# Talking-heads attention and two MLPs on one core: one shuffle transfer for each block of ten tokens, loads issued by GpSimd, deeper weight buffers

## The chip, the core and the metric

The kernel runs on one core of a Trainium2 chip. The metric is the device time of one execution, in microseconds. TensorE (PE) multiplies, VectorE (DVE), ScalarE (ACT) and GpSimd (POOL) work on tiles, and SyncE (SP) issues transfers. Each engine executes its own instructions in program order; transfers run on 16 DMA engines.

## The reference, cut to what matters

```python
def _attn_ref(q, k, v, w_pre, w_post):          # 4 batches, 12 heads, 448 tokens, 64 wide
    scores = scale * np.matmul(q, k.transpose(0, 1, 3, 2))
    scores = np.einsum('bhij,hg->bgij', scores, w_pre)     # mixes the heads
    scores = scores - np.max(scores, axis=-1, keepdims=True)
    attn = np.exp(scores)
    attn = attn / (np.sum(attn, axis=-1, keepdims=True) + 1e-09)
    attn = np.einsum('bhij,hg->bgij', attn, w_post)        # mixes the heads again
    return np.matmul(attn, v)
# x = attention output as (1792, 768); then
# _moe_ref:  h = x @ w_in (768x1024); h * softmax(h); layer norm; @ w_out
# _moe2_ref: relu(x @ w_in (768x2048))**2 @ w_out
```

## The kernel before, in words

The program has three parts: attention, the first MLP and the second MLP. The change touches attention, and the conversion of the first MLP's weights that is interleaved with it.

**Chunks and blocks.** The 448 tokens of a batch are cut into chunks of 120, 120, 120 and 88. A chunk's scores are computed for one pair of heads at a time (`qk`, six calls a chunk): tokens go to partitions 0 to 59 (first half of the chunk) and 64 to 123 (second half), and ACT copies the result to `ssrc`, whose row on a partition holds 12 heads by 448 keys. To mix the heads, partitions must become (token, head) pairs. So `shuffle` sends a block of ten tokens (`R = 10`) from `ssrc` to a tile `sdst`: five tokens of the first half by one transfer of 60 rows, five of the second half by another. Each row is 448 float32. A slot treats two blocks. There are 180 blocks and 90 slots.

**A slot s** issues, in this order: the loads whose turn it is (k, q, v, raw weights), the shuffles of slot s+5 (`DS = 5`), stores of converted weights, `pre(s+2)` on PE (the first head mix), `post_out(s-1)` on DVE (from PSUM to `at`), `qk` for a later chunk, `negmax` and `expo` of slot s+2, `av` (the product with v) where a chunk has just been completed, `weigh(s+1)` (the reciprocal of the sums on DVE, the scaled weights `w` on GpSimd), and `post(s)` on PE (the second head mix). `qk`, `av` and `post` share two PSUM buffers, `ring`.

**Weights.** `load_w1` fetches 48 pieces of 128 by 256 int64 words to `w1raw` (3 buffers). `narrow` turns a piece into float32 with one ACT instruction (L76) and four DVE instructions (L77, L81, L85, L89); they are placed singly between the other DVE instructions by `filler()`. The result is in `w1t` (3 buffers), from which `store_w1` sends it to DRAM. Every load, shuffle and store above is issued by SP. A piece i is loaded in slot (3i+7)//2, its conversion is queued in slot (3i+8)//2, and its store is issued in slot (3i+16)//2.

**Startup.** GpSimd clears small tiles, among them `wz`, which 16 warm-up matmuls read; then come the six `qk` of the first chunk.

Of the kernel before, what the change touches and what calls it, by code (L numbers as in the profile page):

```python
# [18 lines left out]
def kernel(  # L19
# [40 lines left out]
    w1iD = dram.tile([DM, F1], F32, name="w1iD")  # L60
    w1oD = dram.tile([F1, DM], F32, name="w1oD")

    mask_sb = const.tile([128, RH], F32, name="mask_sb")
    wp_raw = const.tile([128, H], F32, name="wp_raw")
    wq_raw = const.tile([128, H], F32, name="wq_raw")
    wpre_bd = const.tile([128, 64], F32, name="wpre_bd")
# [59 lines left out]
    blocks = []  # L126
    for b in range(B):
        for (i0, n) in CHUNKS:
            c, nb, oa = len(chunks), -(-n // R), 0
            chunks.append(dict(b=b, i0=i0, n=n, first=len(blocks), nb=nb))  # L130
            for k in range(nb):
                r = len(range(k, n, nb))
                blocks.append((c, k, r, oa))
                oa += r
# [13 lines left out]
    def load_k(b, g):  # L148

        t = early_p.tile([128, KG, S], F32, tag=f"k{g}", name="k", bufs=2)  # L150
        src = kT[b].rearrange("p (a d) s -> d (p a) s", a=2)
        for e in range(2):
            o = e * HP + KG * g
            nc.sync.dma_start(out=t[64 * e:64 * e + 64], in_=src[:, o:o + KG])
        kk[b, g] = t

    def load_q(c):
# [9 lines left out]
    def load_v(b, j):  # L167
        if j < NJ:
            t = late_p.tile([JW, H, D], F32, tag=f"v_{j}", name="v", bufs=2)
            nc.sync.dma_start(out=t, in_=v[b, j * JW:(j + 1) * JW].rearrange("j (g d) -> j g d", g=H))  # L170
        else:
            t = late_p.tile([128, 2, G2, D], F32, tag=f"v_{j}", name="v", bufs=2)
            src = v[b, j * JW:S].rearrange("j (e g d) -> e j g d", e=2, g=G2)
            for e in range(2):
                nc.gpsimd.memset(t[64 - 64 * e:128 - 64 * e, e], 0.0)
            for e in range(2):
                nc.sync.dma_start(out=t[64 * e:64 * e + 64, e], in_=src[e])
        vv[b, j] = t

    def qk(c, p, dve=0):  # L180


        ch = chunks[c]
        n, half = ch["n"], RH * ch["nb"]
        if c not in ssrc:
            ssrc[c] = ss_p[c % 2].tile([128, H, S], F32, tag="ssrc", name="ssrc")
        ps = ring()
        k = kk[ch["b"], p // KG]
        for x in range(2):
            for e in range(2):  # L190
                u = x ^ e
                nc.tensor.matmul(  # L192
                    out=ps[64 * u:64 * u + 64, e, 0:S],
                    lhsT=qq[c][64 * e:64 * e + 64, p * n + u * half:p * n + u * half + 64],
                    rhs=k[64 * e:64 * e + 64, p % KG],
                    start=True,
                    stop=True,
                )
        (nc.vector.tensor_copy if dve else nc.scalar.copy)(ssrc[c][:, p:H:HP, :], ps[:, :, 0:S])  # L199

    def rows(t, u):

        return H * (RH if u == 0 else blocks[t][2] - RH)

    def shuffle(t):
        c, k, r, oa = blocks[t]
        nb = chunks[c]["nb"]
        d = late_p.tile([128, S], F32, tag="sdst", name="sdst", bufs=10)
        for u in range(2):
            m = rows(t, u)  # L210
            o = 64 * (u ^ (t % 2))
            f = 64 * u + k
            nc.sync.dma_start(out=d[o:o + m], in_=ssrc[c][f:f + (m // H - 1) * nb + 1:nb])
        sdst[t] = d
# [7 lines left out]
    def pre(s):  # L222

        ps = [psb_p.tile([128, 512], F32, tag="pre", name="ps_pre", bufs=4) for b in range(2)]
        ds = [sdst.pop(2 * s + b) for b in range(2)]
        for b, r in ((0, 0), (0, 1), (1, 0), (1, 1)):
            u = r ^ b
            m = rows(2 * s + b, u)
            nc.tensor.matmul(  # L229
                out=ps[b][64 * u:64 * u + 64, 0:S],  # L230
                lhsT=wpre_bd[64 * r:64 * r + m],
                rhs=ds[b][64 * r:64 * r + m],
                start=True,
                stop=True,
            )
        pres[s] = ps
# [41 lines left out]
    def post(s):  # L278

        ps = ring()  # L280
        w = ws.pop(s)
        for b in range(2):
            e = es.pop((s, b))
            for j in range(NJ + 1):
                for x in range(2):
                    for u in range(2):
                        c = x ^ u
                        m = rows(2 * s + b, u)
                        o = j * JW + c * 64 if j < NJ else NJ * JW
# [11 lines left out]
    def post_out(s, b):
        c, k, r, oa = blocks[2 * s + b]
        ps = pps[s] if b == 0 else pps.pop(s)
        if c not in at:
            at[c] = late_p.tile([128, NU, 120], F32, tag="at", name="at", bufs=2)
        nc.vector.tensor_copy(  # L306
            at[c][:, :, oa:oa + R].rearrange("p n (u i) -> p u n i", u=2),
            ps[:, :, b * NU * RH:(b + 1) * NU * RH].rearrange("p u (n i) -> p u n i", i=RH),
        )

    def av(c, a):

        ch = chunks[c]
        n, nb = ch["n"], ch["nb"]
# [16 lines left out]

        kf = n - (R - 1) * nb
        pv = ps[:, 0, 0:360].rearrange("p (q t) -> p q t", q=3)
        for k0, k1, i1 in ((0, kf, R), (kf, nb, R - 1)):
            if k0 == k1:
                continue
            o = k0 * R
            nc.scalar.copy(
                xt[c][:, 3 * a:3 * a + 3, 0:i1 * nb].rearrange("p q (i k) -> p q k i", k=nb)[:, :, k0:k1],
                pv[:, :, o:o + (k1 - k0) * i1].rearrange("p q (k i) -> p q k i", i=i1),  # L340
            )
        if a == 1:
            at.pop(c)

# [15 lines left out]

    def load_w1(i):
        src, dst, k, o = w1pieces[i]
        t = raw_p.tile([128, WP], I64, tag="w1raw", name="w1raw", bufs=3)
        nc.sync.dma_start(out=t, in_=src[k * 128:(k + 1) * 128, o:o + WP])
        w1raw[i] = t

    def narrow_w1(i):
        src, dst, k, o = w1pieces[i]
        sq = raw_p.tile([128, WP], F32, tag="w1sq", name="w1sq", bufs=1)
        t = raw_p.tile([128, WP], F32, tag="w1t", name="w1t", bufs=3)  # L370
        yield from narrow(w1raw.pop(i), sq, t)
        if dst is w1oD:
            nc.scalar.activation(out=t, in_=t, func=AF.Copy, scale=g_sb[:, k:k + 1])
# [86 lines left out]
    nc.gpsimd.memset(mask_sb, 0.0)  # L460
    nc.gpsimd.memset(wp_raw, 0.0)
    nc.gpsimd.memset(wq_raw, 0.0)
    for u in range(2):
        nc.sync.dma_start(out=mask_sb[64 * u:64 * u + PR], in_=mask[0:PR, 0:RH])
        nc.sync.dma_start(out=wp_raw[64 * u:64 * u + PR], in_=w_pre.unsqueeze(0).to_broadcast([RH, H, H]))
    load_q(1)
    for u in range(2):
        nc.sync.dma_start(out=wq_raw[64 * u:64 * u + PR], in_=w_post.unsqueeze(0).to_broadcast([RH, H, H]))

    def consts():  # L470
# [3 lines left out]
        nc.vector.tensor_tensor(  # L474
            out=wpre_bd[:, 0:PR].rearrange("p (i g) -> p i g", g=H),
            in0=wp_raw.unsqueeze(1).to_broadcast([128, RH, H]),
            in1=mask_sb.unsqueeze(2).to_broadcast([128, RH, H]),
            op=ALU.mult,
        )
        nc.vector.tensor_tensor(  # L480
            out=wpost_bd,
            in0=wq_raw.unsqueeze(2).to_broadcast([128, H, RH]),
            in1=mask_sb.unsqueeze(1).to_broadcast([128, H, RH]),
            op=ALU.mult,
        )

# [502 lines left out]
```

## Time and profile before

| | |
|---|---|
| median of 3 runs | 1217.07 us (1215.13 to 1221.67) |
| the profiled execution: time, span | 1219.8 us, 1218.0 us |
| mean granted TensorE clock | 0.943 of full speed |
| PE, DVE, ACT, GpSimd busy, share of the span | 90%, 58%, 39%, 17% |
| attention | about the first 480 us |
| the two MLPs | the rest; PE is busy nearly all of it |

An engine's busy share is an average over the whole span, and the parts differ. What a change in attention is worth has to be read from that part alone, by the waits inside it.

### The profile page before, as it was taken

To read this page: it belongs to the slowest core of one execution; us is meant where nothing else is said; L and a number is where in the kernel's file an instruction comes from. 1 tells how busy PE (TensorE), PEld (TensorE's weight loads), DVE (VectorE), ACT (ScalarE), POOL (GpSimd) and SP (SyncE) were. 2 spreads that over 40 slices of the span, in tenths; PEclk is the share of its full clock that TensorE was granted. 3 is DMA by queue.
4 is the path that set the end of the run, shared out by engine and by line. 5 is a ranking of instruction groups with operands and counts; after the bars stand their busy time and mean duration, and the time that the engine had idled before them with its cause. 6 is when DMAs were issued, how large, how long until landed. Compare 5 with 4: busy or idle time off the path is not lost.

```text
span 1218.0 us, 31090 instructions
## 1 busy us (share of the span) xinstructions
PE 1099.0 (90%) x12920; PEld 937.2 (77%) x12920; DVE 710.8 (58%) x1419; ACT 473.8 (39%) x1033; POOL 211.3 (17%) x362
## 2 busy tenths in 40 slices
PE   8587877776786797999999999999999999999998
PEld 2354544454454475788899899999999999999998
DVE  2465755565566665483344268737676766666734
ACT  4354545455555555342122135633223232232211
POOL 0101111011111125260111035401111111111100
PEclk8878988888989896999999999999999999999999
DMA  4565556455655545231111046402111112111113
GB/s 138 166 187 175 171 185 190 161 170 187 195 168 190 175 148 186 71 98 46 52 48 38 20 150 193 125 27 66 53 52 53 53 52 60 54 57 52 40 66 117
DMA packets 103895, 135.01 MB, mean 111 GB/s; under 512 B 21835, under 2 KB 87243, under 8 KB 103755
## 3 DMA queue, kind: packets, MB, share of 16 engines
q1 hardware_dynamic: 102154, 132.38, 34.6%
q8 instruction: 102, 1.67, 0.6%
q10 hardware_dynamic: 1600, 0.64, 0.2%
q14 instruction: 39, 0.31, 0.1%
HBM read 71.65 MB, written 22.81 MB: 78 GB/s over the span
## 4 chain that ended last, share of the span: by engine, by line
PE 56%; DVE 1%; DMA 1%; ACT 0%; POOL 0%; issue 0%; SPq 0%; DVEq 0%; POOLq 0%
PE ps_h L853 19%; PE ps_y L892 19%; PE ps_o L699 10%; PE ps_h L429 8%; PE ps_tr L685 1%; DMA x2r<-x2D 1%; DMA xD<-xt 0%; DVE e L668 0%; PE ps_ye L892 0%; ACT x L762 0%; ACT y L901 0%; DVE x L764 0%; DVE st L661 0%; DVE e L658 0%; POOL x L764 0%
## 5 line engine op out<-in xcount | busy, mean ns | idle before, releaser
L853 PE MATMUL ps_h<-x,ti 128*128 128x384 f32 (+1 forms) x1440 | 241.9, 325 | 0.0
L892 PE MATMUL ps_y<-to,g 128*128 128x384 f32 x1332 | 240.7, 337 | 0.9 <-ACT y L901 0.9
L853 PEld LDWEIGHTS ps_h<-x,ti 128*128 128x128 f32 x1440 | 236.8, 188 | 0.0
L892 PEld LDWEIGHTS ps_y<-to,g 128*128 128x128 f32 x1332 | 232.5, 188 | 3.0 <-DVE y L903 1.7
L292 PEld LDWEIGHTS ps_ring<-w,e 60*64 60x64 f32 (+1 forms) x5760 | 104.4, 144 | 95.9 <-issue 65.5
L292 PE MATMUL ps_ring<-w,e 60*64 60x60 f32 (+2 forms) x5760 | 111.9, 228 | 49.7 <-DVE at L306 30.0
L306 DVE COPY at<-ps_ring 128x420 f32<-128x420 f32 x180 | 105.1, 605 | 87.4 <-PE ps_ring L292 86.7
L192 PE MATMUL ps_ring<-k,q 64*64 64x448 f32 x768 | 109.6, 602 | 50.2 <-DVE at L306 49.1
L199 ACT COPY ssrc<-ps_ring 128x896 f32<-128x896 f32 x93 | 84.2, 906 | 127.1 <-PE ps_ring L192 99.0
L247 ACT ACTIVATE e<-ps_pre,nm 128x448 f32<-128x448 f32 x180 | 113.4, 637 | 45.7 <-DVE nm L240 43.6
L861 ACT ACTIVATE r<-ps_h 128x384 f32<-128x384 f32 (+1 forms) x80 | 37.5, 469 | 214.1 <-PE ps_h L853 214.0
L699 PE MATMUL ps_o<-zt,w1o 128*128 128x384 f32 (+1 forms) x720 | 120.2, 326 | 0.0
L429 PE MATMUL ps_h<-w1i,xs 128*128 128x512 f32 x504 | 120.1, 395 | 0.0
L324 PEld LDWEIGHTS ps_ring<-at,v 128*64 128x64 f32 x1536 | 89.9, 158 | 35.6 <-issue 21.4
L699 PEld LDWEIGHTS ps_o<-zt,w1o 128*128 128x128 f32 x720 | 117.1, 189 | 0.0
L240 DVE TENSOR_REDUCE nm<-ps_pre 128x1 f32<-128x448 f32 x180 | 107.3, 613 | 12.9 <-PE ps_pre L229 12.9
L862 DVE SCALAR_TENSOR_TENSOR r<-ps_h,r 128x384 f32<-128x384 f32 (+1 forms) x80 | 42.4, 530 | 122.6 <-ACT r L861 122.6
L192 PEld LDWEIGHTS ps_ring<-k,q 64*64 64x64 f32 x768 | 35.0, 145 | 101.8 <-issue 77.5
L264 POOL TENSOR_TENSOR w<-wpost_bd,sm 128x60 f32<-128x60 f32 x166 | 44.3, 288 | 389.1 <-DVE sm L259 202.0
L903 DVE TENSOR_TENSOR y<-ps_y,y 128x768 f32<-128x768 f32 x97 | 92.4, 952 | 32.0 <-PE ps_y L892 32.0
L229 PE MATMUL ps_pre<-sdst,wpre_bd 60*64 60x448 f32 x720 | 106.2, 603 | 4.8 <-DMA sdst<-ssrc 4.0
L429 PEld LDWEIGHTS ps_h<-w1i,xs 128*128 128x128 f32 x504 | 94.1, 188 | 21.3
(77 smaller groups left out, 1064.8 us busy)
## 6 DMA issues: line engine op xcount, KB each, us to landing
sdst<-ssrc SPq DMA_DIRECT2D x352, 105.0 KB
wr<-in_moe_w_in_dram SPq DMA_DIRECT2D x32, 384.0 KB
wr<-in_moe_w_out_dram SPq DMA_DIRECT2D x32, 384.0 KB
w1raw<-in_moe_w_in_dram SPq DMA_DIRECT2D x24, 256.0 KB
w1raw<-in_moe_w_out_dram SPq DMA_DIRECT2D x24, 256.0 KB
k<-in_kT_dram SPq DMA_DIRECT2D x24, 224.0 KB
out_dram<-y SPq DMA_DIRECT2D x13, 384.0 KB
v<-in_v_dram SPq DMA_DIRECT2D x12, 384.0 KB
```

Of the source, the lines that this page charges most:

```text
L192: nc.tensor.matmul(out=ps[64 * u:64 * u + 64, e, 0:S], lhsT=qq[c][64 * e:64 * e + 64, p * n + u * half:p * n + u * half + 64], rhs=k[64 * ...
L229: nc.tensor.matmul(out=ps[b][64 * u:64 * u + 64, 0:S], lhsT=wpre_bd[64 * r:64 * r + m], rhs=ds[b][64 * r:64 * r + m], start=True, stop=True,)
L240: nc.vector.tensor_reduce(out=nm, in_=pres[s][b][:, 0:S], op=ALU.max, axis=AX.X, negate=True)
L247: nc.scalar.activation(out=e, in_=pres[s][b][:, 0:S], func=AF.Exp, bias=nms.pop((s, b)), scale=1.0, accum_out=sms[s][:, b:b + 1])
L292: nc.tensor.matmul(out=ps[64 * c:64 * c + 64, u, i0:i0 + ng * RH], lhsT=e[64 * u:64 * u + m, o:o + 64], rhs=w[64 * u:64 * u + m, b, g0:g0 ...
L306: nc.vector.tensor_copy(at[c][:, :, oa:oa + R].rearrange("p n (u i) -> p u n i", u=2), ps[:, :, b * NU * RH:(b + 1) * NU * RH].rearrange(" ...
L324: nc.tensor.matmul(out=ps[64 * e:64 * e + 64, 0, q * 120:q * 120 + n], lhsT=t[:, g] if j < NJ else t[:, e, p], rhs=at[c][:, j * H + (g if ...
L429: nc.tensor.matmul(out=ps[:, u], lhsT=t[:, a, cc], rhs=w1i[cc][:, w, u * 512:(u + 1) * 512], start=(cc == 0 and a == 0 and w == 0), stop=( ...
L699: nc.tensor.matmul(out=ps[:, 0:width], lhsT=w1o[k][:, w, cc * 128:(cc + 1) * 128], rhs=zT[:, a, k, 0:width], start=(k == 0 and i == 0), st ...
L853: nc.tensor.matmul(out=ps[:, 0:n], lhsT=ti[:, w, cc, f * 128:(f + 1) * 128], rhs=x2[q][:, a, cc], start=(cc == 0 and i == 0), stop=(cc == ...
L892: nc.tensor.matmul(out=ps[:, u - us[0], 0:DM // 2], lhsT=g[:, a, f, o:o + 128], rhs=to[:, w, f, u * (DM // 2):(u + 1) * (DM // 2)], start= ...
L903: nc.vector.tensor_tensor(out=yo, in0=po, in1=yo, op=ALU.add)
```

## The change

A block's ten tokens now come from one half of a chunk. A block therefore needs one transfer of 120 rows, from ten partitions of `ssrc` to partitions 4 to 123 of `sdst`. Rows 0 to 3 are cleared once for ten fixed tiles, and the first head mix reads 64 rows instead of 60 for one of its two products. Because the place of the tokens in PSUM after `post` is another, `post_out` copies one bank for both blocks of a slot instead of both banks for one block, and `av` orders its output accordingly; where two blocks differ in chunk or size, `post_out` makes two copies of half the size. The loads of v, of the raw weights, and of k from the second batch on are issued by GpSimd. `w1raw` has 5 buffers instead of 3, `w1t` 6 instead of 3, and a piece is loaded two or three slots earlier, in slot (3i+2)//2.

```diff
+            n0 = 60 if n == 120 else 50
+            for u, m in enumerate((n0, n - n0)):
+                nk = -(-m // R)
+                for k in range(nk):
+                    r = len(range(k, m, nk))
+                    blocks.append((c, 64 * u + k, nk, r, oa))
...
-            nc.sync.dma_start(out=t[64 * e:64 * e + 64], in_=src[:, o:o + KG])
+            (nc.gpsimd if b else nc.sync).dma_start(out=t[64 * e:64 * e + 64], in_=src[:, o:o + KG])
...
-            nc.sync.dma_start(out=t, in_=v[b, j * JW:(j + 1) * JW].rearrange("j (g d) -> j g d", g=H))
+            nc.gpsimd.dma_start(out=t, in_=v[b, j * JW:(j + 1) * JW].rearrange("j (g d) -> j g d", g=H))
...
+    gaps = []
+    for i in range(10):
+        d = late_p.tile([128, S], F32, name=f"sdst{i}")
+        nc.gpsimd.memset(d[0:4], 0.0)
+        gaps.append(d)
...
     def shuffle(t):
-        c, k, r, oa = blocks[t]
-        nb = chunks[c]["nb"]
-        d = late_p.tile([128, S], F32, tag="sdst", name="sdst", bufs=10)
-        for u in range(2):
-            m = rows(t, u)
-            o = 64 * (u ^ (t % 2))
-            f = 64 * u + k
-            nc.sync.dma_start(out=d[o:o + m], in_=ssrc[c][f:f + (m // H - 1) * nb + 1:nb])
+        c, f, nk, r, oa = blocks[t]
+        d = gaps[t % 10]
+        nc.sync.dma_start(out=d[4:4 + r * H], in_=ssrc[c][f:f + (r - 1) * nk + 1:nk])
         sdst[t] = d
...
-            m = rows(2 * s + b, u)
+            m = H * size(2 * s + b, 1) if r else 64
...
+    def post_out(s, u):
+        ps = pps[s] if u == 0 else pps.pop(s)
+        pv = ps[:, u, 0:2 * NU * RH].rearrange("p (b n i) -> p b n i", b=2, i=RH)
+        two = [blocks[2 * s + b] for b in range(2)]
...
+        if c0 == c1 and r0 == r1 == R:
+            dst = at[c0][:, :, oa:oa + 2 * R].rearrange("p n (x i) -> p x n i", i=RH)
+            nc.vector.tensor_copy(dst[:, 1:3] if u else dst[:, 0:4:3], pv)
+        else:
+            for b, (c, f, nk, r, oa) in enumerate(two):
+                g = u ^ b
+                m, o = size(2 * s + b, g), oa + RH * g
+                nc.vector.tensor_copy(at[c][:, :, o:o + m], pv[:, b, :, 0:m])
...
-        t = raw_p.tile([128, WP], I64, tag="w1raw", name="w1raw", bufs=3)
-        nc.sync.dma_start(out=t, in_=src[k * 128:(k + 1) * 128, o:o + WP])
+        t = raw_p.tile([128, WP], I64, tag="w1raw", name="w1raw", bufs=5)
+        nc.gpsimd.dma_start(out=t, in_=src[k * 128:(k + 1) * 128, o:o + WP])
...
-        t = raw_p.tile([128, WP], F32, tag="w1t", name="w1t", bufs=3)
+        t = raw_p.tile([128, WP], F32, tag="w1t", name="w1t", bufs=6)
...
-        at_slot((3 * i + 7) // 2, load_w1, i)
+        at_slot((3 * i + 2) // 2, load_w1, i)
```

Where the instructions stand now: on SP, in the first batch (`sdst` is a shuffle, `w1iD<-w1t` a store of converted weights, `xD<-xt` a store of the attention output). Before:

```order
L213 DMA sdst<-ssrc 60x1x448 x4
L350 DMA xD<-xt 64x6x120 x2
L164 DMA q<-in_qT_dram 64x720 x2
L364 DMA w1raw<-in_moe_w_in_dram 128x256
L213 DMA sdst<-ssrc 60x1x448 x4
L381 DMA w1iD<-w1t 128x256
```

The same place with the change:

```order
L401 DMA w1iD<-w1t 128x256
L214 DMA sdst_94<-ssrc 120x1x448
L214 DMA sdst_96<-ssrc 120x1x448
L370 DMA xD<-xt 64x6x120 x2
L168 DMA q<-in_qT_dram 64x720 x2
L214 DMA sdst_98<-ssrc 120x1x448
L214 DMA sdst_100<-ssrc 120x1x448
L401 DMA w1iD<-w1t 128x256
```

Four shuffles a slot have become two, and the loads of raw weights have left this queue.

On GpSimd, in the middle of the first batch (`w` are the scaled weights of the second head mix), before:

```order
L264 TENSOR_TENSOR w<-wpost_bd,sm 128x60 x2
L175 MEMSET v 64x384 x2
L264 TENSOR_TENSOR w<-wpost_bd,sm 128x60 x10
L161 MEMSET q 128x64
L264 TENSOR_TENSOR w<-wpost_bd,sm 128x60 x10
```

With the change:

```order
L179 MEMSET v 64x384 x2
L181 DMA v<-in_v_dram 64x384 x2
L269 TENSOR_TENSOR w<-wpost_bd,sm 128x60 x2
L384 DMA w1raw<-in_moe_w_in_dram 128x256
L269 TENSOR_TENSOR w<-wpost_bd,sm 128x60 x2
L158 DMA k<-in_kT_dram 64x2x448 x2
L384 DMA w1raw<-in_moe_w_in_dram 128x256
L269 TENSOR_TENSOR w<-wpost_bd,sm 128x60 x2
```

One to three transfers now stand ahead of a slot's two products `w`.

On GpSimd at the start of the program, with the change:

```order
L208 MEMSET sdst_110 4x448
L208 MEMSET sdst_112 4x448
L468 MEMSET wz 128x256
L165 MEMSET q 128x64
L479 MEMSET wpre_bd 128x64
```

Ten clears of 4 by 448 (the last two are shown) now stand ahead of `wz`, which was the first of them before.

## Rows read from the trace of the kernel before

**Rows 1.** Stretches of the span: busy time and instructions of each engine, clock, DMA share.

```profile
core 0: us, PE busy (x) PEld busy (x) DVE busy (x) ACT busy (x) POOL busy (x), PEclk, DMA share, GB/s
14.00:26.00 12.00, 9.82 (x52) 2.91 (x52) 3.06 (x8) 4.53 (x8) 0.00 (x0) 0.72 0.30 109
...
14.00:478.00 464.00, 352.36 (x8344) 225.84 (x8344) 270.05 (x727) 245.75 (x567) 62.93 (x207) 0.86 0.55 175
...
498.00:1218.00 720.00, 714.50 (x4112) 689.38 (x4106) 427.98 (x664) 216.49 (x440) 140.05 (x133) 1.00 0.22 69
```

**Rows 2.** Issues on SP by line: count, ns min/median/max, first and last start.

```profile
L213 SPq DMA_DIRECT2D sdst<-ssrc x360: 665/742/881, 13.9 to 470.8; - x180
L364 SPq DMA_DIRECT2D w1raw<-in_moe_w_in_dram x24: 362/522/1540, 42.0 to 227.3; - x24
L154 SPq DMA_DIRECT2D k<-in_kT_dram x24: 607/656/1467, 2.0 to 319.8; - x24
```

**Rows 3.** Timeline of SP's queue, 386 to 396 us: start, duration, what.

```profile
386.09 3.58 SPq L213 DMA_DIRECT2D sdst<-ssrc  x4
389.72 0.47 SPq L381 DMA_DIRECT2D w1oD<-w1t  x1
...
390.89 0.45 SPq L364 DMA_DIRECT2D w1raw<-in_moe_w_out_dram  x1
391.58 3.63 SPq L213 DMA_DIRECT2D sdst<-ssrc  x4
395.26 0.46 SPq L381 DMA_DIRECT2D w1oD<-w1t  x1
```

**Rows 4.** Timeline 395 to 398 us: start, duration, what, idle time before it.

```profile
395.57 0.29 DVE L77 TENSOR_SCALAR w1t<-w1raw 128x256 uint32<-128x256 uint32 x1 [7.26 <-DMA w1oD<-w1t]
...
397.36 1.77 PE L192 MATMUL ps_ring<-k,q 64*64 64x448 f32 x8 [9.35 <-DVE at L306]
```

**Rows 5.** Waits of DVE and ACT for transfers, first 480 us: total, times, longest.

```profile
DVE w1t L77 <- DMA w1oD<-w1t: 33.9, 10, 8.5
DVE w1t L77 <- DMA w1iD<-w1t: 30.2, 7, 6.7
DVE w1t L77 <- DMA w1raw<-in_moe_w_in_dram: 14.9, 3, 8.9
...
ACT ssrc L199 <- DMA sdst<-ssrc: 18.7, 6, 7.9
ACT w1sq L76 <- DMA w1raw<-in_moe_w_in_dram: 16.1, 5, 8.4
ACT w1sq L76 <- DMA w1raw<-in_moe_w_out_dram: 7.9, 4, 4.2
```

**Rows 6.** Timeline of PE, 233 to 243 us, between two stalls.

```profile
233.24 2.68 PE L324 MATMUL ps_ring<-at,v 128*64 128x120 f32 x48
235.85 1.13 PE L292 MATMUL ps_ring<-w,e 60*64 60x60 f32 x64
...
239.64 1.13 PE L292 MATMUL ps_ring<-w,e 60*64 60x60 f32 x64
240.56 0.99 PE L229 MATMUL ps_pre<-sdst,wpre_bd 60*64 60x448 f32 x8
241.34 0.96 PE L192 MATMUL ps_ring<-k,q 64*64 64x448 f32 x8
242.42 1.13 PE L292 MATMUL ps_ring<-w,e 60*64 60x60 f32 x64
```

**Rows 7.** Timeline of the start: GpSimd's first clears and PE's first `qk`.

```profile
0.73 0.31 POOL L448 MEMSET wz<- 128x256 f32 x1 [0.29 <-POOLq L975]
0.97 0.15 POOL L161 MEMSET q<- 128x64 f32 x1
...
6.13 2.17 PE L192 MATMUL ps_ring<-k,q 64*64 64x448 f32 x16
```

**Rows 8.** GpSimd's largest wait, first 480 us: total, times, longest.

```profile
POOL w L264 <- DVE sm L259: 202.0, 39, 13.1
```

More of the change, by code (lines that the diff above doesn't have):

```diff
@@ L61 @@
     w1oD = dram.tile([F1, DM], F32, name="w1oD")
-    mask_sb = const.tile([128, RH], F32, name="mask_sb")
+    mask_sb = const.tile([128, 2, RH], F32, name="mask_sb")
     wp_raw = const.tile([128, H], F32, name="wp_raw")
@@ L128 @@
         for (i0, n) in CHUNKS:
[L129 to L134, printed above, removed]
+            c, oa = len(chunks), 0
+            n0 = 60 if n == 120 else 50
+            chunks.append(dict(b=b, i0=i0, n=n, first=len(blocks), n0=n0))
+            for u, m in enumerate((n0, n - n0)):
[3 more added lines that the diff above has]
+                    blocks.append((c, 64 * u + k, nk, r, oa))
+                    oa += r
+            chunks[c]["nb"] = len(blocks) - chunks[c]["first"]
     NB = len(blocks)
@@ L176, in load_v @@
             for e in range(2):
-                nc.sync.dma_start(out=t[64 * e:64 * e + 64, e], in_=src[e])
+                nc.gpsimd.dma_start(out=t[64 * e:64 * e + 64, e], in_=src[e])
         vv[b, j] = t
@@ L183, in qk @@
         ch = chunks[c]
-        n, half = ch["n"], RH * ch["nb"]
+        n, half = ch["n"], ch["n0"]
         if c not in ssrc:
@@ L199, in qk, with size @@
         (nc.vector.tensor_copy if dve else nc.scalar.copy)(ssrc[c][:, p:H:HP, :], ps[:, :, 0:S])
-    def rows(t, u):
-        return H * (RH if u == 0 else blocks[t][2] - RH)
-    def shuffle(t):
-        c, k, r, oa = blocks[t]
-        nb = chunks[c]["nb"]
-        d = late_p.tile([128, S], F32, tag="sdst", name="sdst", bufs=10)
-        for u in range(2):
-            m = rows(t, u)
-            o = 64 * (u ^ (t % 2))
-            f = 64 * u + k
-            nc.sync.dma_start(out=d[o:o + m], in_=ssrc[c][f:f + (m // H - 1) * nb + 1:nb])
+    gaps = []
[3 more added lines that the diff above has]
+        gaps.append(d)
+    def shuffle(t):
+        c, f, nk, r, oa = blocks[t]
+        d = gaps[t % 10]
+        nc.sync.dma_start(out=d[4:4 + r * H], in_=ssrc[c][f:f + (r - 1) * nk + 1:nk])
         sdst[t] = d
+    def size(t, g):
+        return RH if g == 0 else blocks[t][3] - RH
     es = {}
@@ L287, in post @@
                         c = x ^ u
-                        m = rows(2 * s + b, u)
+                        m = H * size(2 * s + b, u ^ b)
                         o = j * JW + c * 64 if j < NJ else NJ * JW
@@ L299, in post @@
         pps[s] = ps
[L301 to L309, printed above, removed]
+    def post_out(s, u):
+        ps = pps[s] if u == 0 else pps.pop(s)
+        pv = ps[:, u, 0:2 * NU * RH].rearrange("p (b n i) -> p b n i", b=2, i=RH)
+        two = [blocks[2 * s + b] for b in range(2)]
+        for c, f, nk, r, oa in two:
+            if c not in at:
+                at[c] = late_p.tile([128, NU, 120], F32, tag="at", name="at", bufs=2)
+        (c0, _, _, r0, oa), (c1, _, _, r1, _) = two
+        if c0 == c1 and r0 == r1 == R:
[6 more added lines that the diff above has]
+                nc.vector.tensor_copy(at[c][:, :, o:o + m], pv[:, b, :, 0:m])
     def av(c, a):
         ch = chunks[c]
-        n, nb = ch["n"], ch["nb"]
+        n = ch["n"]
         if c not in xt:
@@ L330, in av @@
                     )
-        kf = n - (R - 1) * nb
         pv = ps[:, 0, 0:360].rearrange("p (q t) -> p q t", q=3)
[L334 to L337, printed above, removed]
+        x = xt[c][:, 3 * a:3 * a + 3]
+        if n == 120:
             nc.scalar.copy(
-                xt[c][:, 3 * a:3 * a + 3, 0:i1 * nb].rearrange("p q (i k) -> p q k i", k=nb)[:, :, k0:k1],
-                pv[:, :, o:o + (k1 - k0) * i1].rearrange("p q (k i) -> p q k i", i=i1),
-            )
+                x.rearrange("p q (u i k) -> p q u k i", u=2, i=R),
+                pv.rearrange("p q (u k i) -> p q u k i", u=2, i=R),
+            )
+        else:
+            for u, m in enumerate((ch["n0"], n - ch["n0"])):
+                nk = -(-m // R)
+                kf = m - (R - 1) * nk
+                for k0, k1, i1 in ((0, kf, R), (kf, nk, R - 1)):
+                    if k0 < k1:
+                        o, z = u * ch["n0"], k0 * R + u * ch["n0"]
+                        nc.scalar.copy(
+                            x[:, :, o:o + i1 * nk].rearrange("p q (i k) -> p q k i", k=nk)[:, :, k0:k1],
+                            pv[:, :, z:z + (k1 - k0) * i1].rearrange("p q (k i) -> p q k i", i=i1),
+                        )
         if a == 1:
@@ L462 @@
     nc.gpsimd.memset(wq_raw, 0.0)
+    nc.sync.dma_start(out=wp_raw[4:4 + 2 * PR], in_=w_pre.unsqueeze(0).to_broadcast([R, H, H]))
     for u in range(2):
-        nc.sync.dma_start(out=mask_sb[64 * u:64 * u + PR], in_=mask[0:PR, 0:RH])
-        nc.sync.dma_start(out=wp_raw[64 * u:64 * u + PR], in_=w_pre.unsqueeze(0).to_broadcast([RH, H, H]))
+        nc.sync.dma_start(out=mask_sb[4 + PR * u:4 + PR * u + PR, 0], in_=mask[u * PR:(u + 1) * PR, u * RH:(u + 1) * RH])
     load_q(1)
     for u in range(2):
+        nc.sync.dma_start(out=mask_sb[64 * u:64 * u + PR, 1], in_=mask[u * PR:(u + 1) * PR, u * RH:(u + 1) * RH])
         nc.sync.dma_start(out=wq_raw[64 * u:64 * u + PR], in_=w_post.unsqueeze(0).to_broadcast([RH, H, H]))
@@ L476, in consts @@
             in0=wp_raw.unsqueeze(1).to_broadcast([128, RH, H]),
-            in1=mask_sb.unsqueeze(2).to_broadcast([128, RH, H]),
+            in1=mask_sb[:, 0].unsqueeze(2).to_broadcast([128, RH, H]),
             op=ALU.mult,
@@ L482, in consts @@
             in0=wq_raw.unsqueeze(2).to_broadcast([128, H, RH]),
-            in1=mask_sb.unsqueeze(1).to_broadcast([128, H, RH]),
+            in1=mask_sb[:, 1].unsqueeze(1).to_broadcast([128, H, RH]),
             op=ALU.mult,
```

## The prediction

> **What bounds the kernel now.** I read the stretches first, because the busy shares of the whole span mix parts with different limits. From 498 us to the end PE is busy for 714.5 of 720 us at full clock; nothing in the change touches that part, so I leave its time as it is. From 14 to 478 us PE is busy for 352 of 464 us at 0.86 of the clock, DVE for 270, ACT for 246 and GpSimd for 63 [rows 1]. No engine is full there, so something else sets the pace, and the waits must say what.
>
> DVE stands still for 33.9 + 30.2 + 14.9 = 79.0 us at the first instruction of a weight conversion (L77): for the store that still reads the output buffer, or for the raw piece. ACT waits 16.1 + 7.9 = 24.0 us for raw pieces and 18.7 us to overwrite `ssrc`, which a shuffle still reads [rows 5]. All are waits for transfers. One of them, followed through: SP issues four shuffles at 386.1 us, the store at 389.7, then goes on without a gap [rows 3]. The store's buffer is needed for the conversion three pieces on, half a slot later in program order. DVE gets it at 395.57, 5.9 us after the issue and after 7.26 us of idleness; `post_out` stands behind that conversion, PE's two ring buffers wait for `post_out`, and PE is idle for 9.35 us. Then `qk` takes 1.77 us [rows 4] instead of 0.96 [rows 6]: that is the pace of the lower of the clock's two levels, after the pause.
>
> Why are the transfers late? Two resources are full. The first is SP's queue. Its 360 shuffles at 742 ns are 267 us, the 48 raw pieces at 522 ns 25 us, and the 38 loads of k and v that the change moves 25 us if each costs k's 656 ns [rows 2]. The rest on this queue (q, outputs, stores, reloads; some 138 issues) is about 72 us, an estimate by the 522 ns of the nearest row. That makes 389 of 464 us, and in the stretch of rows 3 hardly 0.1 us lies between two issues.
>
> The second is a part of the DMA engines. Between 14 and 26 us almost only shuffles move, back to back, and the DMA share is 0.30, which is 4.8 of 16 engines, at 109 GB/s [rows 1]. A five-token transfer reads five partitions; so it looks as if five engines carry it. All shuffles of the kernel are 38.5 MB (180 blocks of up to 120 rows of 1792 bytes): 353 us at 109 GB/s. All other traffic is the remaining share, 0.55 - 0.30 x 353 / 464 = 0.32 of 464 us, or 149 us on each engine if it is spread evenly. 353 + 149 = 502 us of work for the five engines in a stage of 464: they are full, within what such a reckoning can tell.
>
> **The change part by part.** *One shuffle a block.* 180 issues go. I take the 120-row transfer at the same 742 ns, since the time is that of an instruction and the row nearest to it has half the rows; the bounds are 522 ns (a 128-row piece) and 1484 ns (twice as much) [rows 2]. SP's shuffles then take 134 us (94 to 267). If ten source partitions mean ten engines, the shuffles load these with 353 / 2 + 149 = 326 us.
>
> The Trainium skill ("DMA: Bandwidth & Descriptors", the section on why a DMA increments its semaphore by 16) says that a transfer runs on the largest number of engines up to 16 that divides the slowest dimension of both sides. That would be five before, as the share of 0.30 suggests, and ten after, which no run here shows yet. By it the engines' sum is the one above; without it, that of the second rival below.
>
> *Loads on GpSimd.* 86 issues (48 + 38) leave SP, 50 us. SP is left with 134 + 72 = 206 us, and no longer sets the pace. On GpSimd nothing in the trace shows what an issue costs. From below I take SP's 522 ns: 45 us in all. From above I ask what it can bear. In a stage of 372 us GpSimd has 372 - 63 = 309 us free, so up to 3.6 us an issue it still finishes in time. What stands behind the issues on GpSimd are the 166 products `w`, for which `post` on PE waits. They are not ready to run before DVE's reciprocal: GpSimd waits 202 us for it [rows 8]. A transfer issued at the start of a slot falls into this wait, so I cost it at nothing; if the cover is gone, each issue that comes between costs its own length.
>
> *Buffers and lead.* With 6 `w1t` the store has about five slots instead of half a slot; with 5 `w1raw` and the earlier load a raw piece has two or three slots. At about 4 us a slot (372 / 90) both are above the 5.9 us of the example. So the 79.0 us of DVE go, and ACT's 24.0 too. The 18.7 us at `ssrc` shrink, but need not vanish: the shuffle is issued only a slot before.
>
> *Clears at the start.* Ten clears stand ahead of `wz`, so also ahead of the warm-up matmuls and the first `qk`, which ran at 6.13 with no wait shown. `wz` with 256 columns holds GpSimd for 0.24 us, from its start to the next [rows 7]; 448 columns at this rate are 0.42 us, ten of them 4.2 us, and at nothing per clear 0. I take 4, on the path.
>
> *Copies.* `post_out` makes 156 copies of full size and 40 of half size instead of 180; the short chunk's output needs three ACT copies instead of two. Both sums are about equal on engines with free time: nothing.
>
> **The sum.** The waits give 79.0 us if ACT's lie inside those of DVE, and 79.0 + 24.0 + 18.7 = 121.7 us if none does. A second way: the time of an undisturbed slot. From one `post` to the next it is 2.78 us (post 0.92, pre 0.78, qk 1.08), and an `av` adds 2.61 [rows 6]. 90 slots of post and pre, 90 `qk`, 24 `av` of 120 tokens and 8 of 88 (1.9, scaled) are 153 + 97 + 63 + 15 = 328 us, so at most 136 us can go. I take 92, nearer to the lower end: DVE's 270 us must fit into the shorter stage (73% of 372), and short waits of PE for DVE, ACT and the products `w` will show where the long ones stood. The stage is then 372 us. From the profiled execution's 1219.8 us I take 92 and add 4: 1131.8. The median of the runs lies 2.7 us under that execution; I forecast 1130 us.
>
> **The rivals.** *SP stays near its limit* (the 120-row issue takes 1484 ns). 267 + 72 = 339 us of issues, and a few per cent of gaps make about 350. Stores and shuffles are late again now and then, the deeper buffers take most of it, the stage is about 395: 1153. For it: the issue may wait for full rings. Against it: a 128-row piece is issued in 522 ns. 10%.
>
> *The shuffle still uses five engines.* Then they are full as before at 502 us of work, and only stalls of the conversion go, to come back as waits for `sdst`: 1205 to 1217. For it: no row shows ten. 6%.
>
> *All waits vanish and PE runs at its undisturbed pace.* Stage 332, just above the 328: 1219.8 - 132 + 4 - 2.7 = 1089. Against it: with DVE at 270 of 332 us PE would have to wait for it nowhere. 10%.
>
> *GpSimd becomes late in part.* Issues of 1 to 3 us fall between reciprocal and `w` in a third of the 86 cases, some 60 us: 1190; half of that: 1160. 10%.
>
> *GpSimd is the bound, and the kernel slower.* From 3.6 us an issue on, each further 0.1 us costs 8.6 us; at (464 - 63) / 86 = 4.7 us the stage is as long as now, and from 4.8 us the kernel is slower by over 0.5%. DVE's two-input conversions run beside these issues and could hold them up; nothing in the trace shows it, and it would need nine times SP's 522 ns. 4%.
>
> The Trainium skill ("SBUF — State Buffer", the box on the "DVE blocks DMA" trap) speaks for these two: GpSimd writes its descriptors through a port that VectorE locks in some of its modes, and a transfer of 620 ns took 3100 ns beside such copies. By that, 86 issues would be 267 us, and with GpSimd's 63 us 330 of 372: late at times, but not the bound. No run here shows it yet.
>
> **How the numbers follow.** The forecast, 1105 to 1155, has the remaining 60%. The range must leave out no more than two in ten: it goes from 1088, the undisturbed pace, to 1180, which takes in SP's rival and half of GpSimd's. About 0.5% is what a measurement can tell from no change. Faster: 60 + 10 + 10 + 10 and part of the five-engine case, 0.92. Same: the rest of that case, 0.04. Slower: 0.04.
>
> **What would show it.** Right: L77's waits for stores and raw pieces fall from 79 to under 10 us; the shuffle's issue stays under 0.9 us; shuffles alone show a DMA share near 0.6; the clock of the stage rises; the first `qk` starts near 10 us; the part with the two MLPs stays at about 720 us. Wrong: a longer issue on SP, `post` waiting for `w` for more than 40 us in all, or PE waiting for `sdst`. The prediction fails if a GpSimd issue takes over 3.6 us, or if the long waits only move to `ssrc` and `sdst`.

## The result and the profile after

The changed kernel takes 1147.28 us, the median of 4 runs (1142.16 to 1153.04), against 1219.15 us for the kernel before in the same comparison. The ratio is 0.9415, with a 95% interval of 0.936 to 0.9469. The profiled execution took 1146.49 us, with a span of 1144.7 us: 73 us less than the one of before. Two single runs below, one of the buffers alone (2401 us) and one with q, k and v earlier (1327 us), were slow and are left out of the medians.

The stretches of the changed kernel's span, to be held against [rows 1] (the columns are the same; the first row is a stretch in which almost only shuffles move, the second is attention, the third the MLPs):

```profile
18.00:26.00 8.00, 5.05 (x36) 1.53 (x36) 1.25 (x2) 1.71 (x2) 0.00 (x0) 0.75 0.55 162
14.00:408.00 394.00, 332.36 (x8378) 215.52 (x8380) 273.12 (x756) 244.40 (x575) 111.48 (x295) 0.94 0.71 206
428.00:1144.00 716.00, 712.12 (x4094) 687.49 (x4092) 426.32 (x664) 216.25 (x438) 139.38 (x133) 1.00 0.23 69
```

The same work in attention (8344 and 8378 PE records) takes 394 instead of 464 us. Its clock rose from 0.86 to 0.94, and the DMA share from 0.55 to 0.71. The MLPs kept their time but for 2 us: from the end of the last `av` to the end of the span it is 719.4 us before and 717.5 us now. So nearly the whole difference lies in attention, where the prediction had put it. Shuffles by themselves now use 0.55 of the 16 engines, 8.8, where it was 4.8.

DVE's largest waits in the changed kernel, first 410 us, to be held against [rows 5]:

```profile
DVE at L316 <- PE ps_ring L297: 90.9, 39, 6.7
DVE ssrc L203 <- PE ps_ring L196: 13.9, 3, 11.7
DVE nm L245 <- PE ps_pre L234: 10.1, 9, 4.3
DVE w1i L436 <- DMA wraw<-w1iD: 7.9, 3, 4.0
DVE sm L262 <- ACT e L252: 4.6, 2, 3.8
```

The 79.0 us of L77 are gone from the list. On ACT the waits for raw pieces (24.0 us) are gone too, and the wait at `ssrc` has shrunk from 18.7 to 10.5 us:

```profile
ACT ssrc L203 <- DMA sdst<-ssrc: 10.5, 2, 5.6
```

What the issues cost now, to be held against [rows 2] (count, ns min/median/max, first and last start):

```profile
L214 SPq DMA_DIRECT2D sdst<-ssrc x180: 768/825/2102, 17.3 to 398.6; - x180
L384 POOL DMA_DIRECT2D w1raw<-in_moe_w_in_dram x24: 536/579/745, 32.4 to 181.8; - x24
L158 POOL DMA_DIRECT2D k<-in_kT_dram x18: 587/616/644, 58.7 to 274.0; - x18
L401 SPq DMA_DIRECT2D w1iD<-w1t x24: 423/948/2162, 58.3 to 214.1; - x24
```

A shuffle of 120 rows is issued in 825 ns, not twice 742. A load costs GpSimd 0.55 to 0.62 us, some 50 us for 86.

The start, to be held against [rows 7]: the ten clears, and the first `qk`.

```profile
0.73 4.17 POOL L208 MEMSET sdst<- 4x448 f32 x10 [0.29 <-POOLq L996]
...
9.90 1.74 PE L196 MATMUL ps_ring<-k,q 64*64 64x448 f32 x16
```

### The profile page after: what moved, and what is told of

Same layout as the page of the kernel before. It is cut to its first block, busy times and chain, and to the rows that moved or that the text cites. A ratio compares the mean times of both kernels' runs of the same rounds, so it can differ in the third digit from the quotient of the medians.

```text
span 1144.7 us, 30947 instructions
## 1 busy us (share of the span) xinstructions
PE 1072.9 (94%) x12920; PEld 923.8 (81%) x12920; DVE 709.3 (62%) x1443; ACT 471.3 (41%) x1041; POOL 262.3 (23%) x458
## 4 chain that ended last, share of the span: by engine, by line
PE 83%; DVE 9%; issue 3%; DMA 2%; ACT 1%; POOL 0%; SPq 0%; POOLq 0%; DVEq 0%; ACTq 0%
PE ps_h L874 21%; PE ps_y L913 20%; PE ps_o L720 10%; PE ps_h L449 10%; PE ps_ring L336 7%; PE ps_ring L297 5%; PE ps_ring L196 4%; PE ps_pre L234 3%; DVE at L316 3%; DVE nm L245 2%; DMA sdst<-ssrc 1%; PE ps_tr L706 1%; DVE at L321 1%; DVE w1t L81 1%; DVE w1t L89 1%
## 5 line engine op out<-in xcount | busy, mean ns | idle before, releaser
L297 PEld LDWEIGHTS ps_ring<-w,e 60*64 60x64 f32 (+1 forms) x5760 | 101.1, 138 | 72.6 <-issue 40.9
L316 DVE COPY at<-ps_ring 128x420 f32<-128x420 f32 x156 | 91.9, 611 | 93.0 <-PE ps_ring L297 92.6
L297 PE MATMUL ps_ring<-w,e 60*64 60x60 f32 (+2 forms) x5760 | 108.6, 222 | 28.7 <-issue 13.8
L196 PE MATMUL ps_ring<-k,q 64*64 64x448 f32 x768 | 104.1, 576 | 23.4 <-issue 11.3
L336 PEld LDWEIGHTS ps_ring<-at,v 128*64 128x64 f32 x1536 | 78.9, 143 | 32.1 <-issue 11.7
L234 PE MATMUL ps_pre<-sdst,wpre_bd 64*64 64x448 f32 x720 | 101.2, 588 | 3.2 <-DMA sdst<-ssrc 3.2
```

What stands on the lines that cost most here:

```text
L196: nc.tensor.matmul(out=ps[64 * u:64 * u + 64, e, 0:S], lhsT=qq[c][64 * e:64 * e + 64, p * n + u * half:p * n + u * half + 64], rhs=k[64 * ...
L234: nc.tensor.matmul(out=ps[b][64 * u:64 * u + 64, 0:S], lhsT=wpre_bd[64 * r:64 * r + m], rhs=ds[b][64 * r:64 * r + m], start=True, stop=True,)
L297: nc.tensor.matmul(out=ps[64 * c:64 * c + 64, u, i0:i0 + ng * RH], lhsT=e[64 * u:64 * u + m, o:o + 64], rhs=w[64 * u:64 * u + m, b, g0:g0 ...
L316: nc.vector.tensor_copy(dst[:, 1:3] if u else dst[:, 0:4:3], pv)
L336: nc.tensor.matmul(out=ps[64 * e:64 * e + 64, 0, q * 120:q * 120 + n], lhsT=t[:, g] if j < NJ else t[:, e, p], rhs=at[c][:, j * H + (g if ...
```

## The experiments

Times are medians; ratios are against the kernel before, run beside them. The kernel with half the columns leaves out half of the scores; all others compute the whole.

| | time, us | ratio (95% interval) |
|---|---|---|
| changed kernel | 1147.3 | 0.9415 (0.936 to 0.9469) |
| changed kernel, second comparison | 1148.1 | 0.9431 (0.9401 to 0.9462) |
| buffers and lead alone | 1210.6 | 0.9941 (0.9919 to 0.9963) |
| buffers, lead and GpSimd's loads, old shuffle | 1210.8 | 0.9941 (0.9925 to 0.9957) |
| new shuffle alone | 1177.6 | 0.966 (0.9628 to 0.9693) |
| new shuffle and GpSimd's loads, old buffers | 1187.1 | 0.975 (0.9713 to 0.9788) |
| new shuffle and buffers, loads on SP | 1167.8 | 0.958 (0.9543 to 0.9617) |
| changed, each shuffle as two transfers | 1179.2 | 0.9676 (0.9654 to 0.9697) |
| changed, half the columns shuffled | 1117.4 | 0.9178 (0.9151 to 0.9205) |
| changed, q, k, v earlier | 1150.4 | 0.9456 (0.9418 to 0.9495) |
| changed, clears later | 1140.4 | 0.9373 (0.9352 to 0.9393) |
| clears later, shuffles on SP and GpSimd in turn | 1151.8 | 0.947 (0.944 to 0.9501) |
| clears later, loads on ACT | 1150.3 | 0.9455 (0.9432 to 0.9478) |

**Buffers and lead alone.** To the kernel before:

```diff
-        t = raw_p.tile([128, WP], I64, tag="w1raw", name="w1raw", bufs=3)
+        t = raw_p.tile([128, WP], I64, tag="w1raw", name="w1raw", bufs=5)
...
-        t = raw_p.tile([128, WP], F32, tag="w1t", name="w1t", bufs=3)
+        t = raw_p.tile([128, WP], F32, tag="w1t", name="w1t", bufs=6)
...
-        at_slot((3 * i + 7) // 2, load_w1, i)
+        at_slot((3 * i + 2) // 2, load_w1, i)
```

> The kernel before with the change's weight buffers (5 raw, 6 converted) and the earlier raw load only; four shuffles a slot and all loads stay on SP. Theory (SP's queue and five DMA engines are full, 389 of 464 us and 502 of 464 us by the prediction's sums): the waits of L77 for stores and raw pieces fall from 79 us to under 15, but the time only comes back as other waits for transfers, and the kernel lands at 1195 to 1217 us. Rival (the lack of buffers alone held the stage): 1219 less 79 us, 1135 to 1160 us.

It took 1210.6 us. L77 waits for no transfer any more, and yet only 7 us are gained. ACT's waits for transfers in its trace (the four largest of seven rows) show where the rest went:

```profile
ACT ssrc L199 <- DMA sdst<-ssrc: 24.5, 5, 8.9
ACT ssrc L199 <- DMA w1raw<-in_moe_w_in_dram: 21.0, 2, 12.7
ACT ssrc L199 <- DMA w1iD<-w1t: 11.0, 1, 11.0
ACT ssrc L199 <- DMA w1oD<-w1t: 10.5, 1, 10.5
```

ACT may not overwrite `ssrc` before a shuffle has read it, and stands there for 67 us in these rows and 89 us in all seven, where it was 20 us before (the rows name the transfer that landed last; the line waits for `ssrc`). The late transfers were the cause, and the wait of DVE only the place where they first showed.

**Everything but the shuffle.** The same with the loads of k, v and raw weights issued by GpSimd:

```diff
-            nc.sync.dma_start(out=t[64 * e:64 * e + 64], in_=src[:, o:o + KG])
+            (nc.gpsimd if b else nc.sync).dma_start(out=t[64 * e:64 * e + 64], in_=src[:, o:o + KG])
...
-        nc.sync.dma_start(out=t, in_=src[k * 128:(k + 1) * 128, o:o + WP])
+        nc.gpsimd.dma_start(out=t, in_=src[k * 128:(k + 1) * 128, o:o + WP])
```

> The kernel before with the change's buffers, earlier raw load and loads on GpSimd, but with its two transfers of 60 rows a block. SP is relieved of 86 issues (some 50 us of 389). Theory (five engines are full as well as SP, 502 us of work by the prediction's sum): SP shows gaps, yet the kernel gains little over the buffers alone (1211): 1192 to 1212 us. Rival (only SP's issues were full): 50 us less issue time in a stage of 464 brings 1155 to 1175 us.

It took 1210.8 us, no less than the buffers alone. ACT's waits at `ssrc` are as long, 86 us in all; the largest row:

```profile
ACT ssrc L199 <- DMA sdst<-ssrc: 71.4, 8, 13.3
```

Between the first and the last shuffle SP is now busy with issues for 341 of 445 us (0.77), where it was 384 of 445 (0.86) with the buffers alone. 86 issues fewer on SP are worth nothing while the shuffles run in the old form. The rival that only SP's issues were full falls.

**The new shuffle alone.** The changed kernel with 3 and 3 buffers, the old load slot, and all loads on SP (the edits above, undone).

> The changed kernel with the old weight buffers, the old raw load slot and all loads on SP: one shuffle a block is all that is left of the change. Theory: queue and engines are free, but a store still has half a slot, so about half of L77's waits stay: 1165 to 1190 us. Rival (the queue alone was the cause of the late stores): within 8 us of the changed kernel, 1139 to 1155. Rival (buffers alone): 1205 to 1220.

It took 1177.6 us. DVE still waits 40 us at L77:

```profile
DVE w1t L77 <- DMA w1oD<-w1t: 19.7, 6, 6.6
DVE w1t L77 <- DMA w1iD<-w1t: 15.2, 7, 7.1
DVE w1t L77 <- DMA w1raw<-in_moe_w_in_dram: 5.2, 1, 5.2
```

So the shuffle is the largest part, and by itself it halves the waits that the buffers take away.

**New shuffle and GpSimd's loads, old buffers.**

> The changed kernel with 3 raw and 3 converted buffers and the old raw load slot; loads stay on GpSimd. Theory (half a slot is too short for a store or a raw load that lands after 3 to 7 us): L77 and the ACT instruction L76 wait again, 40 to 70 us in all, 1175 to 1205 us. Rival (buffers do not matter on free queues): 1139 to 1155 us.

It took 1187.1 us, 10 us more than with the loads on SP. The waits have moved to the raw pieces. These rows are DVE's and ACT's:

```profile
DVE w1t L77 <- DMA w1raw<-in_moe_w_in_dram: 20.8, 8, 4.3
DVE w1t L77 <- DMA w1oD<-w1t: 10.5, 4, 4.0
DVE w1t L77 <- DMA w1raw<-in_moe_w_out_dram: 8.9, 5, 3.3
...
ACT w1sq L76 <- DMA w1raw<-in_moe_w_in_dram: 16.5, 8, 3.7
ACT w1sq L76 <- DMA w1raw<-in_moe_w_out_dram: 11.0, 8, 3.2
```

A raw piece that GpSimd loads half a slot ahead is late; with two or three slots ahead it is not.

**New shuffle and buffers, loads on SP.**

> The changed kernel with all loads of k, v and raw weights back on SP. SP then has 180 x 0.825 us of shuffles and some 224 other issues at 0.5 to 0.9 us, 260 to 350 of a stage of about 392 us. Theory (the move to GpSimd was not needed once the shuffles were halved): within 8 us of the changed kernel, 1139 to 1155 us. Rival (SP's issue time still counts): 1160 to 1185 us. Rival (loads issued by GpSimd cost something, by slower packets or by GpSimd's time): 1125 to 1138 us.

It took 1167.8 us, 20 us more than the changed kernel. The rival, that SP's issue time still counts, holds. SP's issues of stores and of v in this kernel:

```profile
L401 SPq DMA_DIRECT2D w1iD<-w1t x24: 443/780/1326, 66.7 to 223.0; - x24
...
L174 SPq DMA_DIRECT2D v<-in_v_dram x12: 487/1030/1922, 39.7 to 355.1; - x12
```

and the wait that this makes for ACT:

```profile
ACT ssrc L203 <- DMA sdst<-ssrc: 43.3, 6, 9.8
```

Between the first and the last shuffle SP issues for 359 of 402 us (0.89); with the loads on GpSimd it is 282 of 381 (0.74). An issue is not a fixed price: this store took 417 ns before. The DMA share alone does not set it, as the next two experiments show: 467 ns at a share of 0.67 with each shuffle as two transfers, 454 ns at 0.60 with half the columns. The long issues stand only in runs whose shuffles move 210 KB an issue; why is not shown.

**Each shuffle as two transfers.** The same ten partitions and bytes, 224 columns each:

```diff
-        nc.sync.dma_start(out=d[4:4 + r * H], in_=ssrc[c][f:f + (r - 1) * nk + 1:nk])
+        for o in (0, S // 2):
+            nc.sync.dma_start(out=d[4:4 + r * H, o:o + S // 2], in_=ssrc[c][f:f + (r - 1) * nk + 1:nk, :, o:o + S // 2])
```

> The changed kernel with each shuffle sent as two transfers of 224 columns: the same ten source partitions and bytes, twice the issues and twice the rows, of half the length. Theory A (SP's issues were one of the two full resources): 360 issues at 0.75 to 0.83 us fill SP again, about 270 to 300 us of shuffles and 100 of the rest, 1170 to 1205 us. Theory B (only the count of engines mattered, five before and ten now): not over 1160 us, the shorter rows costing a few us.

It took 1179.2 us, 31 us more than the changed kernel. The issues, as forecast by theory A, are 360 x 0.773 = 278 us:

```profile
L215 SPq DMA_DIRECT2D sdst<-ssrc x360: 768/773/1822, 17.8 to 433.1; - x180
```

SP issues for 370 of 415 us (0.89) here. That the rows are half as long explains little: the DMA engines' packets took 38.5% of the span of 1179.8 us, 454 us, against 39.0% of 1144.7, 446 us. So more engines are not enough: both halves of the new shuffle, the spread and the single issue, are needed. The stores on SP:

```profile
L402 SPq DMA_DIRECT2D w1iD<-w1t x24: 368/467/2237, 72.2 to 235.6; - x24
```

**Half the columns.** Only columns 0 to 223 are shuffled, and half of the scores are left out; every engine's instructions stay, but for larger clears at the start.

```diff
-        nc.gpsimd.memset(d[0:4], 0.0)
+        nc.gpsimd.memset(d, 0.0)
...
-        nc.sync.dma_start(out=d[4:4 + r * H], in_=ssrc[c][f:f + (r - 1) * nk + 1:nk])
+        nc.sync.dma_start(out=d[4:4 + r * H, 0:S // 2], in_=ssrc[c][f:f + (r - 1) * nk + 1:nk, :, 0:S // 2])
```

> The changed kernel with shuffles of the first 224 of 448 columns only (the other half of each sdst tile stays cleared, so half of the scores are left out); the count of issues and every engine's instructions stay. Theory (ten DMA engines are nearly full again, by 21600 rows x 0.094 us / 10 + 159 us of other traffic = 362 of 392 us, and loads, stores and PE's instruction refills come late through them): half the bytes free the engines, the pauses of PE in the middle of a line go, and the stage comes near the undisturbed pace: 1100 to 1128 us. Rival (PE, DVE and ACT hold each other up, transfers no longer matter): 1138 to 1155 us.

It took 1117.4 us, 30 us less. Its attention, as a stretch:

```profile
14.00:378.00 364.00, 318.22 (x8380) 208.71 (x8378) 273.74 (x755) 244.27 (x576) 111.09 (x295) 0.99 0.60 170
```

The clock is at 0.99 and PE is busy for 318 us, close to the 328 us that the prediction took as the undisturbed pace. So the shuffled bytes still cost the changed kernel some 30 us, by the engines or by SP, whose issues fall to 216 of 353 us as well; this run does not part the two. But the stage takes 364 us even so, 36 more than 328, and nothing here puts those down to transfers.

**q, k and v earlier.**

```diff
-                    at_slot(s - 5, load_k, ch["b"], p // KG)
+                    at_slot(s - 8, load_k, ch["b"], p // KG)
...
-                at_slot(beg - 2, load_q, c)
+                at_slot(beg - 4, load_q, c)
...
-                at_slot((ch["first"] + 1) // 2 + (3 if c == 0 else 0) + j, load_v, ch["b"], j)
+                at_slot((ch["first"] + 1) // 2 - (0 if c == 0 else 0) + j, load_v, ch["b"], j)
```

> The changed kernel with q loaded two slots and k three slots earlier and the first batch's v three slots earlier. Theory (what is left are transfers on full engines and PE's instruction refills, not the place of these loads): 1140 to 1152 us. Rival (the pauses of PE at qk and av are q, k or v that come late): 1120 to 1137 us.

It took 1150.4 us in runs from 1142 to 1158; its interval overlaps that of the changed kernel. It shows no gain, so the rival of late loads falls. The trace of the changed kernel agrees: PE waits there 2.2 us for v, and not at all for q and k.

**Clears later, and the changed kernel again.** The clears of the ten tiles stand behind the other clears of the start:

```diff
-        nc.gpsimd.memset(d[0:4], 0.0)
...
     nc.gpsimd.memset(wq_raw, 0.0)
+    for d in gaps:
+        nc.gpsimd.memset(d[0:4], 0.0)
```

> The changed kernel with the ten clears of sdst behind the other clears of the start instead of ahead of them. By the trace, the clears hold GpSimd for 4.17 us and the first qk starts at 9.90 instead of 6.13 us. Theory (this is on the path): 3 to 5 us less than the changed kernel, 1139 to 1146 us. Rival (the delay is caught up later in the stage): no difference.

> The changed kernel once more, to have its time beside more runs: 1142 to 1150 us. If the version with later clears is really 4 us faster, this ratio lies at 0.940 to 0.943, above that version's 0.9373.

1140.4 against 1148.1 us. The two intervals do not touch; that of the first comparison of the changed kernel (0.936 to 0.9469) does overlap. In the trace the first `qk` starts at 5.92 instead of 9.90 us. So the 4 us at the start are on the path, and this is the best of the versions that compute the whole; what it gains beyond 4 us is not explained.

**Shuffles on SP and GpSimd in turn** (with later clears):

```diff
-        nc.sync.dma_start(out=d[4:4 + r * H], in_=ssrc[c][f:f + (r - 1) * nk + 1:nk])
+        (nc.gpsimd if t % 2 else nc.sync).dma_start(out=d[4:4 + r * H], in_=ssrc[c][f:f + (r - 1) * nk + 1:nk])
```

> The changed kernel with the clears behind the others, and every second shuffle issued by GpSimd instead of SP. If a transfer issued by GpSimd is not bound to the same ten engines, the load spreads over all sixteen. Theory (the ten engines are nearly full, and that is what is left): pauses of PE and waits at ssrc shrink, 1120 to 1137 us. Rival (GpSimd's order: a shuffle that waits for ssrc holds back the products w behind it): 1145 to 1180 us.

It took 1151.8 us, 11 us more than its own base. The theory that spreading helps falls, and the rival's reason isn't seen either: PE waits 13.0 us for `w`, against 11.0 in the base, and GpSimd stands once for `ssrc`, at the start. What grew in the trace are PE's pauses without a releaser, from 24 to 31 us. This is its `post`, first in the base (clears later) and then here:

```profile
PE ps_ring L293 <- issue: 17.1, 9, 3.5
...
PE ps_ring L293 <- issue: 22.6, 15, 3.9
```

That is not the whole 11 us: the traced run took 1143.8 us, the shortest of its four, against 1139.5 us for the base's.

**Loads on ACT** (with later clears): `nc.scalar` instead of `nc.gpsimd` in the loads.

> The changed kernel with later clears, and the 86 loads issued by ACT instead of GpSimd, so that they keep their place off SP but go through a hardware queue as SP's do. Theory (the pauses of PE in the middle of a line, 25 us in the changed kernel and 2 us before, are instruction refills held up by the transfers that GpSimd issues: they are 5 us with the buffers alone and 10 us with the loads on GpSimd added): these pauses fall under 12 us, 1120 to 1137 us. Rival 1 (they come from the load on the DMA engines, whoever issues): pauses of 20 to 30 us, 1137 to 1147 us. Rival 2 (86 issues of 0.5 to 1 us on ACT's path cost more than they save): 1148 to 1175 us.

It took 1150.3 us. The pauses did fall, to 13.0 us in all (8.8 at `post`), nearly to the theory's 12, but the time is rival 2's. The 86 issues take 49 us on ACT's queue, and ACT waits in its order; in the base the first of these rows is 9.4 us and the second is not there:

```profile
ACT ssrc L203 <- DMA sdst<-ssrc: 22.6, 8, 4.8
...
ACT ssrc L203 <- DMA k<-in_kT_dram: 18.2, 4, 6.2
```

## Why the prediction was right, and where it was off

**Two full resources: right.** Each relieved alone gives little or only part. With the buffers, the lead and GpSimd's loads in place: SP's 86 issues fewer give nothing with the old shuffle (1210.6 and 1210.8), ten engines with 360 issues (and the rest of the new shuffle's code) 32 us (1210.8 to 1179.2), and the single issue another 31 us (1179.2 to 1148.1). SP's issues took 390 of the 457 us from the first to the last shuffle before (0.85), close to the 389 of the sum. Which engine moved a packet is not in the trace; that five and then ten are in use is read from the shares of 0.30 and 0.55.

**The 120-row issue: right in size.** 825 ns against 742 taken. *SP no longer sets the pace with 206 us*: right in what follows, wrong in size. SP's issues take 282 of the 381 us from the first to the last shuffle. The step behind the 206, that an issue has a fixed time, failed: stores went from 417 to 948 ns, and with the loads kept on SP it is a limit again. The first rival's stage of 395 us lies near the measured 394, but not by its reason: its issue of 1484 ns is 825 in the median, and its 339 us of issues are 282.

The Trainium skill ("DMA: Bandwidth & Descriptors", the section on issuing engines not being separate DMA queues) says that issuing from several engines only saves the sequencer's issue time, usually small beside the transfer. Here the trace differs in size, and it depends on the rest: the 86 loads off SP are worth 20 us with the whole change (1167.8 to 1148.1), nothing with the old shuffle, and with the new shuffle and the old buffers they cost 10 us (1177.6 to 1187.1).

**Ten engines: right in direction, wrong in size.** 8.8 engines' worth of share, but a rate of 162 GB/s against 109, not twice as much. So the 38.5 MB of shuffles take 238 us and not 353 / 2, and with the 149 us of other traffic the engines hold 387 us of work, not 326, in a stage of 394 (362 by the reckoning recorded with the half columns). They were relieved, but not free.

**GpSimd's issue costs nothing: right for `w`, wrong for PE's pauses** (below). It took 0.58 us; PE's wait for `w` at `post` is 14.3 us in all in the changed kernel, after 14.9 us before:

```profile
PEld ps_ring L292 <- POOL w L264: 14.9, 21, 1.7
...
PEld ps_ring L297 <- POOL w L269: 14.3, 22, 1.7
```

The Trainium skill's warning ("SBUF — State Buffer", the "DVE blocks DMA" trap) does not show in the issues here: the longest of the 86 on GpSimd took 745 ns. The page's 3100 ns, which the prediction multiplied by 86, is the time of a transfer and not of an issue; no run here times a transfer with and without VectorE's copies beside it.

**The waits of L77 and ACT go: right.** 103 us of such waits are gone. That the stage was held by late transfers, and not by a lack of buffers, is shown by the buffers alone.

**The start, 4 us: right.** 9.90 against 6.13 us, and with later clears 5.92.

**The stage of 372 us: off.** The stretch from 14 to 408 us is 394, and it holds the later start, which the sum counted by itself; without it the stage is 390, and 74 us came out of it, not 92. This is the term that was mis-sized: I took 44 us over the undisturbed 328 for short waits of engines on each other; it is 62. Half the shuffled bytes take 30 of these away, so what the sum lacked is a price for these bytes, on engines that are still nearly full and in SP's longer issues. Part of it is a new wait. PE's waits without a releaser, first in the kernel before and then in the changed one:

```profile
PE ps_ring L292 <- issue: 1.5, 2, 0.9
```

```profile
PE ps_ring L297 <- issue: 13.8, 9, 3.4
...
PE ps_ring L196 <- issue: 11.3, 5, 3.0
```

They rose from 2 to 25 us, and some lie in the middle of one run of matmuls, where nothing new is waited for. In the timeline of PE in the changed kernel, one `post` stops after a part of its matmuls and goes on 2.37 us later:

```profile
156.33 0.52 PE L297 MATMUL ps_ring<-w,e 60*64 60x60 f32 x18
159.22 0.80 PE L297 MATMUL ps_ring<-w,e 60*64 60x60 f32 x40 [2.37 <-issue]
```

Counted along PE's records in the trace, 11 of the 21 pauses over 1 us stand at positions 1217, 2497, 5057, 5313, 5825, 7105, 9409, 9666, 11457, 12481 and 15809: all but one exactly, and that one to one record, a multiple of 256 apart. They make 23 of the 44 us of such pauses; before, one of 23 such pauses stood there, with 1 of 94 us. The profile's page has a queue that fetches instructions (packets, MB, share of 16 engines):

```profile
q8 instruction: 102, 1.67, 0.6%
```

102 packets for PE's 26,148 records are one for 256. The times of these packets in the trace agree: from the second boundary up to 410 us, exactly one more packet has ended before each of the 66 boundaries, PE never passes one earlier than 1.3 us after that packet's end, and at the 11 pauses it goes on 1.3 to 1.7 us after it. So PE waits for the next packet of its program. The packets themselves took about as long as before (medians 1.03 and 1.00 us); they come late, and what holds them is not shown.

What the pauses hang on is shown in part. The issuer of the loads counts: in kernels that differ in nothing else they are 5.3 us with SP and 11.5 with GpSimd on the old shuffle, 5.5 and 12.0 on the new shuffle with old buffers, 9.5 and 25.1 on the new shuffle with new buffers (26.1 in the second trace of the changed kernel), and 13.0 with ACT against 23.8 with GpSimd (both with later clears). The shuffled bytes count too: 15 us with half of them. `post` with all loads on SP, to be held against the 13.8 us above:

```profile
PE ps_ring L297 <- issue: 6.9, 8, 1.9
```

So a load issued by GpSimd had a cost that the sum put at nothing, though it is not on GpSimd's path to `w`. What these pauses alone cost stays open, since every edit that cut them changed other waits too.

## What to carry to other kernels

Before giving a stalled engine more buffers, ask why its transfer is late: here buffers and lead alone gave 0.6%; with the transfers made fewer and spread they were worth 39 us with the loads on GpSimd (1187 to 1148) and 10 us with them on SP (1178 to 1168). Count issues on a queue, and engines in flight, as resources of their own; a DMA share of 0.55 on average hid, by the reckoning of the prediction, five engines that were full. When the transfers are spread over more engines, measure their rate before you halve their time: here it rose by half. When an issue carries more bytes, look at the issue times again, and when loads move to another engine, look whether PE pauses on its own instructions.

## What the runs showed of the hardware that I had not expected

A store of 128 rows took SP 417 ns to issue between shuffles of 105 KB an issue and 948 ns between shuffles of 210 KB; with two issues of 105 KB for each block it was 467 ns, though the DMA share was 0.67. PE pauses of 1 to 3.4 us stood a multiple of 256 records apart, each ending 1.3 to 1.7 us after a packet of the instruction queue. With the loads issued by GpSimd instead of SP, PE's pauses without a releaser grew from 5 to 12 us on the old shuffle, at the same DMA share of 0.57.
